# A linear-attention and gated-MLP kernel on one core: decays scanned over whole units, 48-column loads, another layout of x, other fillers on TensorE, and a re-planned order

## The chip, the cores and the metric

The kernel runs on one core of a Trainium2 chip. The metric is the device time of one execution in microseconds; the shown runs of the kernel before took 529.38, 530.78 and 531.95 us, median 530.78.

## The reference

Four batches of eight heads run a recurrence over 768 tokens; its output, laid out as 3072 tokens of 384 features, goes through two matrix products with a piecewise quadratic gate between them.

```python
for t in range(S):
    y[:, :, t] = einsum('bhd,bhde->bhe', rt, state + (u * kt) x vt)
    state = wt[:, :, :, None] * state + kt x vt
x = y.transpose(0, 2, 1, 3).reshape(3072, 384)
h = x @ w_in                                    # 384 -> 2048
g = where(h >= 1, h, where(h <= -1, 0, (h + 1) ** 2 / 4))
out = g @ w_out                                 # 2048 -> 384
```

## The kernel before

**Units.** The tokens are cut into 12 units of 256 (`UT`), three to a batch; a unit is four chunks of 64 (`C`). Two units make a block of 512 tokens, and the products run block by block.

**Attention of a unit** (`attention`). The decays w of a unit come in two halves q (pairs of heads, 128 partitions). For each half VectorE scans w to running products p (L405), takes the reciprocal of the last (L399), scans backwards to y (L400), and multiplies k by y (L428) and r by p (L478). Each chunk of 64 has its own start of the scan. TensorE then multiplies 64x64 tiles: `among` (L448) gives r times k within a chunk, in the first four units a second time with u times k (L416 on GpSimd, `with_u`); `ktrans` (L487) transposes k; `umat` (L509) makes k times v per chunk. VectorE picks masked parts of the `among` products (L454, `picked`), and builds the states at the chunk borders from `umat`: per chunk an add (L527) and a multiply by the chunk's total decay (L528), `chain`. At the end `cross` and `along` (both L550) add up state times r and picked scores times v into two banks of PSUM. ScalarE and VectorE evacuate these into `x` as a high part and a rest (L606, L604), and six small transfers fill in the rows of the last head (L649). Unit 0 has a path of its own (`ALONE`): matmuls L625 and L616 take the place of the transfers and of VectorE's rest.

**Weights.** Each of 16 slices f of the two weight matrices is loaded as 64-bit numbers (768 KB) and decoded: ScalarE (L329, L326, L322), GpSimd (L330, `rr`), VectorE (L332 `fl`, then L335 `wt`, the low part). The tile `rr` exists once, so GpSimd's L330 for one slice waits until VectorE's L332 for the slice before has read it.

**Products.** For every block and slice, nine matmuls of 512 columns make h (L896, `product_in`), five operations on ScalarE and VectorE gate it (L712, L713, L714 `g`, L716 `gh`, L717 `gl`), and nine more add into the output banks (L916, `product_out`, whose last three wait for `gl`). Some steps of the first two blocks run in two halves of 256 columns, so that they can start when only one unit of the block is there: 112 steps in all.

**The order.** Nothing is issued as it is written: every operation is recorded in a `Plan` with an engine, a cost in us, the tiles it touches and a due time. The planner plays a list schedule with these costs and emits all engines' instructions in the order found; each engine then works strictly in that order. Due times come from constants: `LEADS` by unit, `DECODE` for the weights, `STEP`, `FIRST` and `PACED` for the products. `kept_warm` puts matmuls on zeros (L304) into TensorE's queue where the planner sees a gap longer than `IDLE`; `warm` (L298) is eight of these at the start.

Of the kernel before, what the change touches and what calls it, by code (L numbers as in the profile page):

```python
# [26 lines left out]
SEG = 2 * NC * (C + 1)  # L27
# [22 lines left out]
class Plan:  # L50
# [7 lines left out]
    HOP = 0.15  # L58
# [4 lines left out]
    def add(self, engine, cost, emit, due, reads=(), writes=(), port=False, size=0, fresh=True):  # L63
# [37 lines left out]
    def kept_warm(self, order, engine, banks, fill):  # L101
# [4 lines left out]
        for n in order:  # L106
            op = ops[n]
            if op["e"] == engine:
# [8 lines left out]
                free = begin[n] + op["cost"]  # L117
# [3 lines left out]
    def order(self):  # L121
# [24 lines left out]
        while any(open_.values()):  # L146
# [66 lines left out]
STEP, FIRST, PACED = 4.9, 24.0, 4.6  # L213
# [3 lines left out]
def attention_moe(tc, a):  # L217
# [63 lines left out]
    for t, v, name in ((zero, 0.0, "zero"), (seeds, 0.0, "seeds"), (minus_one, -1.0, "minus_one")):  # L281
        op("POOL", 0.5, SOON, (), [name], lambda t=t, v=v: G.memset(t, v))
# [17 lines left out]
    op("PE", 2.0, SOON, ["zero"], [("b", 6)], warm)  # L300
# [8 lines left out]
    def weight(f, when):  # L309
# [20 lines left out]
        op("POOL", 2.0, due, [("raw", f)], ["rr_high"], lambda: G.tensor_scalar(  # L330
# [6 lines left out]
        plan.group(first, when, DECODE)  # L337
# [12 lines left out]
    def attention(u, when):  # L350
# [45 lines left out]
        def scan(q, back):  # L396
            w = wq[slot[q]]
            if back:
                V.reciprocal(seeds[:, :, C], pv[:, q, :, C])  # L399
# [3 lines left out]
            else:  # L403
                V.memset(seeds[:, :, C], 0.0)
# [15 lines left out]
        for q in (1, 0):  # L420
            s = slot[q]
            if early:
                op("POOL", 1.6, due, [("k", s), "cst"], [("ku", q), "nk"], lambda q=q: with_u(q))
            op("DVE", 1.3, due, [("w", s)], [("p", q), "seeds"], lambda q=q: scan(q, False), port=True)
            op("ACT", 0.2, due, [("p", q)], [("ptot", u, q)], lambda q=q: A.copy(
                ptot[:, 16 * u + 8 * q : 16 * u + 8 * q + 8], pv[:, q, :, C]))
            op("DVE", 1.45, due, [("w", s), ("p", q)], ["y", "seeds"], lambda q=q: scan(q, True), port=True)
            op("DVE", 0.69, due, ["y"], [("k", s)], lambda q=q: V.tensor_tensor(  # L428
                out=parts(q, 1), in0=parts(q, 1), in1=y_.rearrange("p (n c) -> p n c", c=C + 1)[:, :, 1:], op=ALU.mult), port=True)
# [47 lines left out]
        for q in (1, 0):  # L477
            op("DVE", 0.69, due, [("p", q)], [("r", slot[q])], lambda q=q: V.tensor_tensor(  # L478
                out=parts(q, 0), in0=parts(q, 0), in1=pv[:, q, :, 0:C], op=ALU.mult), port=True)
# [505 lines left out]
```

## Time and profile before

| | before |
|---|---|
| median of the runs shown | 530.78 us |
| span of the profiled execution | 526.9 us |
| median less this span | 3.9 us |
| TensorE matmuls, busy | 503.0 us, 95% of the span |
| VectorE, busy | 340.4 us, 65% |
| ScalarE, busy | 294.4 us, 56% |
| GpSimd, busy | 108.8 us, 21% |
| transfers, moved | 54.22 MB, mean 103 GB/s |

The profile is of one execution. PE is TensorE's matmuls, PEld its weight loads, DVE VectorE, ACT ScalarE, POOL GpSimd, SP SyncE, which issues the transfers. L numbers are lines of the kernel. A group's row has busy time and mean duration of one, then the idle time of the engine just before these instructions and who ended it. An fp32 matmul of the attention appears as two records, the products' matmuls as one. Matmuls overlap, so a mean duration is longer than the distance from one to the next; the chain of waits shows that distance.

### The profile page before, as it was taken

The page shows a single profiled execution, that of the slowest core. Times are in us where ns is not written, and L with a number is a line of the kernel's source. Part 1 is how long each engine was busy: PE and PEld are TensorE (multiplying, and loading weights), DVE is VectorE, ACT ScalarE, POOL GpSimd, SP SyncE. Part 2 cuts the span into 40 slices and gives each one's busy share as a digit, 9 for nine tenths or more (in the row PEclk, how much of TensorE's full clock was granted, in tenths as well). Part 3 has the DMA queues.
Part 4 walks back from the last instruction along what each step waited for, and adds up shares of the span by engine and source line. Part 5 has one row for each costly group of instructions (what it writes and reads, how often), then busy time and mean ns, then how long its engine had stood idle before and what let it go on. Part 6 is the DMA issues. An engine that isn't in the chain of part 4 may idle for free.

```text
span 526.9 us, 12832 instructions
## 1 busy us (share of the span) xinstructions
PE 503.0 (95%) x5438; PEld 412.2 (78%) x5438; DVE 340.4 (65%) x592; ACT 294.4 (56%) x596; POOL 108.8 (21%) x76
## 2 busy tenths in 40 slices
PE   7778899999999999999999999999999999999993
PEld 5557787788999988887877778887787777788882
DVE  5989799999897868324398869445833545333331
ACT  1387698878786556433464736443744444444441
POOL 6496865740203021000111011101000100000000
PEclk9899999999999999999999999999999999999997
DMA  8865472344835171100234404103200100100001
GB/s 321 344 240 179 152 318 81 122 148 145 271 104 181 44 237 48 61 0 3 82 125 140 151 20 151 56 2 109 78 0 2 41 17 12 66 0 1 0 0 67
DMA packets 21921, 54.22 MB, mean 103 GB/s; under 512 B 3104, under 2 KB 8672, under 8 KB 21856
## 3 DMA queue, kind: packets, MB, share of 16 engines
q1 hardware_dynamic: 21568, 52.93, 29.2%
q8 instruction: 44, 0.72, 0.5%
q10 hardware_dynamic: 288, 0.39, 0.2%
q14 instruction: 21, 0.17, 0.1%
HBM read 46.43 MB, written 4.72 MB: 97 GB/s over the span
## 4 chain that ended last, share of the span: by engine, by line
PE 77%; POOL 6%; DVE 5%; issue 4%; DMA 3%; ACT 1%; SPq 1%; ACTq 0%; DVEq 0%; POOLq 0%
PE h L896 35%; PE acc L916 33%; POOL rr L330 4%; PE bank L550 3%; POOL nk L416 3%; PE bank L509 2%; PE bank L448 2%; PE bank L487 1%; DMA rk<-in_rk 1%; DVE fl L332 1%; SPq L649 1%; DMA cst<-in_consts 1%; DVE y L400 1%; DVE p L405 1%; DVE gl L717 1%
## 5 line engine op out<-in xcount | busy, mean ns | idle before, releaser
L896 PE MATMUL h<-x,wt 128*128 128x512 f32 (+1 forms) x1008 | 223.7, 367 | 2.4 <-DVE wt L335 1.5
L896 PEld LDWEIGHTS h<-x,wt 128*128 128x128 f32 x1008 | 169.6, 188 | 36.2 <-DVE wt L335 2.2
L916 PE MATMUL acc<-gh,wt 128*128 128x512 f32 (+1 forms) x672 | 156.4, 368 | 0.0
L714 DVE SCALAR_TENSOR_TENSOR g<-g,h 128x512 f32<-128x512 f32 (+1 forms) x112 | 67.9, 606 | 99.8 <-ACT g L713 97.5
L916 PEld LDWEIGHTS acc<-gh,wt 128*128 128x128 f32 x672 | 114.0, 188 | 22.1 <-issue 0.5
L712 ACT ACTIVATE g<-h 128x512 f32<-128x512 f32 (+1 forms) x112 | 60.0, 536 | 116.6 <-PE h L896 113.4
L717 DVE TENSOR_TENSOR gl<-g,gh 128x512 fp32r<-128x512 f32 (+1 forms) x112 | 71.5, 640 | 35.6 <-ACT gh L716 35.6
L916 PE MATMUL acc<-gl,wt 128*128 128x512 f32 (+1 forms) x336 | 86.1, 364 | 1.1 <-DVE gl L717 1.1
L716 ACT CAST gh<-g 128x512 fp32r<-128x512 f32 (+1 forms) x112 | 62.2, 556 | 44.4 <-DVE g L714 42.1
L916 PEld LDWEIGHTS acc<-gl,wt 128*128 128x128 f32 x336 | 58.7, 188 | 12.5 <-DVE gl L717 1.5
L713 ACT ACTIVATE g<-g 128x512 f32<-128x512 f32 (+1 forms) x112 | 63.9, 571 | 3.2
L474 POOL TENSOR_TENSOR r<-cst,d 128x512 f32<-128x512 f32 x16 | 16.8, 1070 | 227.5 <-PE bank L550 207.9
L330 POOL TENSOR_SCALAR rr<-wraw 128x768 uint16<-128x768 f32 x16 | 51.6, 3227 | 28.4 <-DVE fl L332 25.1
L405 DVE TENSOR_TENSOR_SCAN p<-wq,seeds 128x520 f32<-128x520 f32 x24 | 30.8, 1283 | 3.1 <-DMA wq<-in_w 2.3
L400 DVE TENSOR_TENSOR_SCAN y<-wq,seeds 128x520 f32<-128x520 f32 x24 | 30.4, 1266 | 0.8
L466 POOL TENSOR_TENSOR nk<-nk 128x768 f32<-128x768 f32 x8 | 15.3, 1914 | 52.5 <-DMA nk<-in_nk 52.5
L416 POOL TENSOR_SCALAR nk<-rk,cst 128x256 f32<-128x256 f32 x16 | 22.5, 1417 | 3.4 <-DMA cst<-in_consts 2.6
L428 DVE TENSOR_TENSOR rk<-rk,y 128x512 f32<-128x512 f32 x24 | 17.9, 745 | 3.6 <-POOL nk L416 2.3
L329 ACT ACTIVATE rr<-wraw 128x768 uint16<-128x768 uint32 x16 | 17.4, 1085 | 1.1 <-DMA wraw<-in_wbits 1.1
L550 PEld LDWEIGHTS bank<-rk,st 64*64 64x64 f32 x656 | 12.3, 134 | 6.9 <-issue 3.7
L454 DVE COPY_PREDICATED r<-below,bank 128x512 f32<-128x512 int32 x22 | 15.1, 727 | 4.0 <-PE bank L448 4.0
L478 DVE TENSOR_TENSOR rk<-rk,p 128x512 f32<-128x512 f32 x24 | 17.4, 736 | 0.3 <-PE acc L448 0.3
(104 smaller groups left out, 398.7 us busy)
## 6 DMA issues: line engine op xcount, KB each, us to landing
rk<-in_rk SPq DMA_DIRECT2D x24, 512.0 KB, 4.6
wraw<-in_wbits SPq DMA_DIRECT2D x16, 768.0 KB, 7.1
wq<-in_w SPq DMA_DIRECT2D x24, 260.5 KB, 2.8
nk<-in_nk SPq DMA_DIRECT2D x8, 768.0 KB, 4.6
vn<-in_v SPq DMA_DIRECT2D x11, 384.0 KB, 6.7
fl<-in_w SPq DMA_DIRECT2D x12, 260.0 KB, 3.1
out_y<-g SPq DMA_DIRECT2D x10, 256.0 KB, 2.5
x<-last SPq DMA_DIRECT2D x66, 32.0 KB, 2.9
```

The lines of the kernel that those rows point to most:

```text
L330: op("POOL", 2.0, due, [("raw", f)], ["rr_high"], lambda: G.tensor_scalar(out=r16[:, :, 1], in0=wraw[f][:, :, 1].bitcast(F32), scalar1=0.0 ...
L400: V.tensor_tensor_scan(out=y_[:, ::-1], data0=w[:, SEG:0:-1], data1=sv[:, ::-1], initial=0.0, op0=ALU.mult, op1=ALU.add)
L405: V.tensor_tensor_scan(out=pv[:, q].rearrange("p n c -> p (n c)"), data0=w[:, 0:SEG], data1=sv, initial=0.0, op0=ALU.mult, op1=ALU.add,)
L416: G.tensor_scalar(out=ku[:, q, cs], in0=rk[slot[q]][:, 1, cs], scalar1=u_col[:, 2 * q + pr : 2 * q + pr + 1], scalar2=None, op0=ALU.mult)
L550: PE.matmul(out=bank[by[g]][HP * half : HP * half + HP, lo : lo + C], start=first, stop=False, skip_group_check=True, **kw)
L712: op("ACT", c, due, [("b", 6 + hk)], [("g", gk)], lambda: nc.scalar.activation(gs, hs, AF.Relu, scale=0.5, bias=0.5))
L713: op("ACT", c, due, (), [("g", gk)], lambda: nc.scalar.activation(gs, gs, AF.Square))
L714: op("DVE", 0.13 + 0.53 * k, due, [("b", 6 + hk)], [("g", gk)], lambda: nc.vector.scalar_tensor_tensor(out=gs, in0=gs, scalar=1.0, in1=hs, ...
L716: op("ACT", c, due, [("g", gk)], [("gh", gk)], lambda: nc.scalar.copy(ghs, gs))
L717: op("DVE", 0.15 + 0.5 * k, due, [("g", gk), ("gh", gk)], [("gl", gk)], lambda: nc.vector.tensor_tensor(out=gls, in0=gs, in1=ghs.bitcast(F ...
L896: nc.tensor.matmul(hp, lhsT=wx[f][:, cs], rhs=xt[:, j, :], start=n == 0, stop=n == 8)
L916: nc.tensor.matmul(o[j], lhsT=wx[f][:, cs], rhs=gt, start=first and i == 0, stop=stop and i == 2, skip_group_check=True)
```

## The change

- **Decays.** The scans start once per unit and pair instead of once per chunk (`SEG` is 514 columns, not 520). The states then need no multiply per chunk: `chain` becomes one add (or one copy), and only the unit's last state is multiplied, by the unit's total (`carry`).
- **48 columns.** The left operands of `umat`, and of `cross` and `along` except in units 0 and 6, are 48 columns instead of 64.
- **x by chunk parity.** Each chunk's results go to a contiguous half of x; the output's tokens are put back in order on the host.
- **Unit 0's u times k** goes from GpSimd to ScalarE, in four instructions.
- **Fillers.** `zeros` and `warm` use an f32r tile `clear`, made by one copy on VectorE, in matmuls of 512 or 256 columns; `warm` is now 48 fp32 matmuls of 64x64 and one f32r matmul for each bank. `IDLE` falls from 1.0 to 0.5, and a gap is filled to 72%.
- **The planner** knows latencies, a price for changing between 64 and 128 row tiles, two rates of transfer; many costs are new, and all due times are.

```diff
-SEG = 2 * NC * (C + 1)
+SEG = 2 * (UT + 1)
-WARM = 8
-IDLE, ZEROS = 1.0, 1.2
+IDLE, FILLED, ZEROS = 0.5, 0.72, 0.235
+SMALL = 48
...
-    HOP = 0.15
+    HOP = 0.04
+    LATENCY = {"PE": 0.16, "DVE": 0.083, "ACT": 0.1}
+    LATE_64 = 0.31
+    TURN = {64: 0.22, 128: 0.09}
+    RATES, SETTLED = (315e3, 400e3), 8.5
...
-SLACK = 1.95
-LEADS = {0: 75.5, 1: 62.4, 2: 17.0, 3: 9.3, 4: 39.0, 5: 15.7, 6: 12.1, 7: 78.9, 8: 43.2, 9: -6.2, 10: 15.7, 11: -1.1}
-LEAD, DECODE = 15, 4.5
+SLACK = 0.501
+LEADS = {0: 89.12, 1: 29.14, 2: 50, 3: 29.29, 4: 70.5, 5: 42.42, 6: 96.05, 7: 79.29, 8: 141.79, 9: 131.35, 10: 73.56, 11: 100.77}
...
-STEP, FIRST, PACED = 4.9, 24.0, 4.6
+STEP, FIRST, PACED, AFTER = 17.0572, 293.658, 16.0129, 4.9
...
+    op("DVE", 0.2, SOON, ["zero"], ["clear"], lambda: V.tensor_copy(clear, zero))
     def warm():
-        for _ in range(WARM):
-            PE.matmul(hp[0][:, 0:128], lhsT=zero, rhs=zero, start=True, stop=True)
+        for n in range(SMALL):
+            g, h = n // 2 % 2, n % 2
+            PE.matmul(bank[h][HP * g : HP * g + C, 0:C], lhsT=zero[HP * h : HP * h + HP, 0:C], rhs=zero[HP * h : HP * h + HP, 0:C],
+                      start=True, stop=True)
+        for b in bank:
+            cleared(b, 4)
+    def cleared(out, n):
+        PE.matmul(out[:, 0 : 128 * n], lhsT=clear, rhs=clear.unsqueeze(1).broadcast_to([128, n, 128]), start=True, stop=True)
     def zeros(b, us):
-        for _ in range(int((us - 0.4) / ZEROS)):
-            PE.matmul(bank[b[1]], lhsT=zero, rhs=zero.unsqueeze(1).broadcast_to([128, 4, 128]), start=True, stop=True)
+        halves = int(FILLED * us / ZEROS * 2)
+        for i in range(0, halves, 2):
+            cleared(bank[b[1]], min(2, halves - i) * 2)
...
-                op("POOL", 1.6, due, [("k", s), "cst"], [("ku", q), "nk"], lambda q=q: with_u(q))
+                if alone:
+                    for pr in range(2):
+                        op("ACT", 0.42, due, [("k", s), "cst"], [("ku", q), "nk"], lambda q=q, pr=pr: A.activation(
+                            ku[:, q, pr * UT : pr * UT + UT], rk[slot[q]][:, 1, pr * UT : pr * UT + UT], AF.Copy,
+                            scale=u_col[:, 2 * q + pr : 2 * q + pr + 1]))
+                else:
+                    op("POOL", 2.85, due, [("k", s), "cst"], [("ku", q), "nk"], lambda q=q: with_u(q))
...
-                            i, o = slice(HP * g, HP * g + HP), slice(HP * h, HP * h + HP)
+                            i, o = slice(HP * g, HP * g + HP), slice(HP * h, HP * h + D)
...
-            V.tensor_tensor(out=sm, in0=up, in1=ss_(old), op=ALU.add)
-            V.tensor_tensor(out=out, in0=sm, in1=pt, op=ALU.mult)
+            if old is None:
+                V.tensor_copy(ss_(new), up(c))
+            else:
+                V.tensor_tensor(out=ss_(new), in0=up(c), in1=ss_(old), op=ALU.add)
+        def carry(new):
+            V.tensor_tensor(out=ss_(new), in0=sm, in1=ptot[:, 4 * u : 4 * u + 4].unsqueeze(2).broadcast_to([128, 4, D]), op=ALU.mult)
...
+        wide = HP if u in INPLACE else D
...
-                to = [x[:, n].rearrange("p a (c g t) -> p a c g t", c=2, g=2)[:, :, :, g, :] for n in range(2)]
+                to = [x[:, n, :, gs].rearrange("p a (c t) -> p a c t", c=2) for n in range(2)]
```

What stands in the queues is shown at three places. A row is line, operation, what is written from what is read, and the shape; the number behind a tile's name is its buffer, for `wraw` the slice f.

GpSimd's queue just behind the memsets of the start, before. `nk` from `rk` and `cst` is u times k of one half of a unit, `rr` from `wraw` is the step of decoding.

```order
L416 TENSOR_SCALAR nk0_84<-rk0_81,cst0_67 128x256 x2
L416 TENSOR_SCALAR nk0_84<-rk1_82,cst0_67 128x256 x2
L330 TENSOR_SCALAR rr0_115<-wraw0_170 128x768
L416 TENSOR_SCALAR nk0_84<-rk2_83,cst0_67 128x256 x2
L330 TENSOR_SCALAR rr0_115<-wraw1_181 128x768
L416 TENSOR_SCALAR nk0_84<-rk0_81,cst0_67 128x256 x2
L330 TENSOR_SCALAR rr0_115<-wraw2_192 128x768
L416 TENSOR_SCALAR nk0_84<-rk1_82,cst0_67 128x256 x2
L330 TENSOR_SCALAR rr0_115<-wraw3_313 128x768
```

The same place now:

```order
L358 TENSOR_SCALAR rr0_116<-wraw0_218 128x768
L358 TENSOR_SCALAR rr0_116<-wraw1_220 128x768
L444 TENSOR_SCALAR nk0_85<-rk2_84,cst0_67 128x256 x2
L358 TENSOR_SCALAR rr0_116<-wraw2_202 128x768
L444 TENSOR_SCALAR nk0_85<-rk0_82,cst0_67 128x256 x2
L358 TENSOR_SCALAR rr0_116<-wraw3_388 128x768
L444 TENSOR_SCALAR nk0_85<-rk1_83,cst0_67 128x256 x2
L358 TENSOR_SCALAR rr0_116<-wraw4_467 128x768
L358 TENSOR_SCALAR rr0_116<-wraw5_488 128x768
```

Unit 0's two rows are gone from the head of the queue, and slices 0 and 1 stand ahead of unit 1's rows.

VectorE's queue where unit 0's states are made, before; `ob`, `g` and `st` hold states, `bank` and `h` are PSUM.

```order
L525 TENSOR_TENSOR ob0_112<-h1_120,ptot0_76 128x4x48
L527 TENSOR_TENSOR sm0_99<-bank2_123,ob0_112 128x192
L528 TENSOR_TENSOR ob0_112<-sm0_99,ptot0_76 128x4x48
L527 TENSOR_TENSOR sm0_99<-h1_120,ob0_112 128x192
L528 TENSOR_TENSOR g2_105<-sm0_99,ptot0_76 128x4x48
L527 TENSOR_TENSOR sm0_99<-bank2_123,g2_105 128x192
L528 TENSOR_TENSOR st1_94<-sm0_99,ptot0_76 128x192
L454 COPY_PREDICATED r0_90<-below0_71,acc2_118 128x512
L454 COPY_PREDICATED r1_91<-below0_71,h0_119 128x512
```

And now:

```order
L488 COPY_PREDICATED r0_91<-below0_71,acc2_119 128x512
L488 COPY_PREDICATED r1_92<-below0_71,h0_120 128x512
L559 COPY ob0_113<-h1_121 128x4x48
L561 TENSOR_TENSOR ob0_113<-bank2_124,ob0_113 128x4x48
L561 TENSOR_TENSOR g2_106<-h1_121,ob0_113 128x4x48
L578 TENSOR_TENSOR sm0_100<-bank2_124,g2_106 128x192
L564 TENSOR_TENSOR st1_95<-sm0_100,ptot0_77 128x192
L360 SCALAR_TENSOR_TENSOR fl0_114<-fl0_114,rr0_116 128x768
```

Five instructions stand for seven, the picking moved ahead of them, and the decoding of slice 0 follows at once, ahead of unit 1's first scan.

TensorE's queue at the start, before:

```order
L298 MATMUL h0_119<-zero0_74 128x128 x8
L304 MATMUL bank0_121<-zero0_74 128x512 x4
L487 MATMUL bank0_121<-cst0_67,rk0_81 128x128 x4
L448 MATMUL acc0_116<-rk1_82,nk0_84 64x64
L448 MATMUL acc1_117<-rk1_82,nk0_84 64x64
```

And now, between the first fillers and the transposes of unit 0, with 46 more small matmuls and seven long ones where lines are left out:

```order
L325 MATMUL bank0_122<-clear0_75 128x512 x2
L319 MATMUL bank0_122<-zero0_74 64x64
L319 MATMUL bank1_123<-zero0_74 64x64
...
L325 MATMUL h1_121<-clear0_75 128x512
L325 MATMUL bank0_122<-clear0_75 128x512 x6
L521 MATMUL bank0_122<-cst0_67,rk0_82 128x128 x4
```

Ahead of the first real matmul stand 48 small and 16 long fillers instead of 8 and 4. In all there are 71 f32r fillers of 512 or 256 columns, 69 of them ahead of unit 2's first matmul; before there were 9 fp32 ones.

More of the change, by code (lines that the diff above doesn't have):

```diff
@@ L116, in kept_warm @@
                             break
-                free = begin[n] + op["cost"]
+                free = end[n] - self.late(op)
             out.append(op["emit"])
@@ L127, in order @@
                 users[m].append(n)
-        free, end, begin, lands = {}, {}, {}, []
+        free, end, begin, lands = {"SP": self.ISSUE}, {}, {}, []
         port = bus = 0.0
-        open_ = {}
+        mode = 128
+        ran = {}
+        open_ = {e: [] for e in ("PE", "SP", "ACT", "DVE", "POOL")}
         since = {}
@@ L135, in opened @@
             op = ops[n]
-            since[n] = max((end[m] + (0.0 if ops[m]["e"] == op["e"] and not ops[m]["size"] else self.HOP) for m in op["deps"]), default=0.0)
-            open_.setdefault(op["e"], []).append(n)
+            since[n] = max((ran[m] if ops[m]["e"] == op["e"] and not ops[m]["size"] else end[m] + self.HOP for m in op["deps"]), default=0.0)
+            open_[op["e"]].append(n)
         def ready(n):
@@ L524, in chain @@
             if old is None:
-                V.tensor_tensor(out=out, in0=up, in1=pt, op=ALU.mult)
-                return
-            V.tensor_tensor(out=sm, in0=up, in1=ss_(old), op=ALU.add)
-            V.tensor_tensor(out=out, in0=sm, in1=pt, op=ALU.mult)
-        for c in range(NC - (third == UB - 1)):
-            old, new = before[-1], (state["st"] + 1) % STATES
-            if alone and c < NC - 1:
+                V.tensor_copy(ss_(new), up(c))
+            else:
+                V.tensor_tensor(out=ss_(new), in0=up(c), in1=ss_(old), op=ALU.add)
@@ L533, in attention @@
+        def carry(new):
+            V.tensor_tensor(out=ss_(new), in0=sm, in1=ptot[:, 4 * u : 4 * u + 4].unsqueeze(2).broadcast_to([128, 4, D]), op=ALU.mult)
+        for c in range(NC - 1):
+            old = before[-1]
+            if alone:
                 new = list(wide_st)[c]
             else:
-                state["st"] = new
-            op("DVE", 0.35 if old is None else 0.71, due, [("b", bu[c % 2]), ("ptot", u, 0), ("ptot", u, 1)] + ([("s", old)] if old is not None else []),
-               [("s", new), "sm"], lambda c=c, old=old, new=new: chain(c, old, new), port=True)
+                new = state["st"] = (state["st"] + 1) % STATES
+            op("DVE", 0.36, due, [("b", bu[c % 2])] + ([("s", old)] if old is not None else []), [("s", new)],
+               lambda c=c, old=old, new=new: chain(c, old, new))
@@ L538, in attention @@
             before.append(new)
+        if third != UB - 1:
+            old = before[-1]
+            new = state["st"] = (state["st"] + 1) % STATES
+            op("DVE", 0.36, due, [("b", bu[1]), ("s", old)], ["sm"], lambda old=old: V.tensor_tensor(
+                out=sm, in0=up(NC - 1), in1=ss_(old), op=ALU.add))
+            op("DVE", 0.36, due, ["sm", ("ptot", u, 0), ("ptot", u, 1)], [("s", new)], lambda new=new: carry(new), port=True)
         by = [take(), take()]
         begun = set()
+        wide = HP if u in INPLACE else D
@@ L549, in put @@
             lo = ((pair // 2 * 2 + h) * 2 + c2) * C
-            PE.matmul(out=bank[by[g]][HP * half : HP * half + HP, lo : lo + C], start=first, stop=False, skip_group_check=True, **kw)
+            PE.matmul(out=bank[by[g]][HP * half : HP * half + wide, lo : lo + C], start=first, stop=False, skip_group_check=True, **kw)
         def inter(g, h, pair, c2):
```

128 lines of the change are left out of this document (70 added, 58 removed).

## The prediction

> **What bounds the kernel now.** I read the busy times by stretches first. The columns are the length, then the busy time of PE, PEld, DVE, ACT and POOL with their instructions, the granted clock, the share of the DMA engines and GB/s.
>
> ```profile
> 0.00:63.20 63.20, 49.15 (x882) 39.00 (x883) 50.29 (x86) 34.59 (x68) 45.20 (x42) 0.97 0.70 257
> 63.20:518.40 455.20, 453.80 (x4558) 373.20 (x4556) 289.65 (x506) 259.03 (x529) 63.64 (x35) 1.00 0.25 82
> 518.40:527.00 8.60, 0.00 (x0) 0.00 (x0) 0.42 (x1) 0.76 (x2) 0.00 (x0) 0.65 0.30 100
> ```
>
> From 63.2 us to 518.4 us TensorE stands for 1.4 us only; then 8.6 us go into the last output. So the end is set by two things: how much of TensorE's queue is done when the start lets go of it, and how long the queue itself is. The prices of its pieces stand in the chain of waits between 160 and 215 us (start, length, what):
>
> ```profile
> 166.01 1.05 PE acc L916 x9
> 167.07 1.09 PE bank L448 x64
> 168.16 1.27 PE acc L916 x9
> 169.43 0.44 PE bank L487 x4
> 173.46 1.08 PE bank L509 x64
> 180.02 0.63 PE bank L550 x32
> 182.96 1.56 PE bank L550 x96
> 191.04 4.21 PE h L896 x18
> ```
>
> A product of nine matmuls costs 1.05 us in half width and 2.1 us in full; the first one behind attention 1.27 us, so a change from 64-row to 128-row tiles costs 0.2 us. A unit's attention is 1.09 (`among`), two times 0.44 (`ktrans`), 1.08 (`umat`), 0.63 (`cross`) and 1.56 us (`along`).
>
> Now the start. The same view by line, up to 63.2 us, gives what TensorE had done; the rows are L896, L916, L448, L487, L509 and L550 in this order (first number: busy PE, in brackets the records). Two rows of the groups by line, for unit 0 alone, follow.
>
> ```profile
> 0.00:63.20 63.20, 10.97 (x72) 9.38 (x73) 0.97 0.70 257
> 0.00:63.20 63.20, 8.44 (x54) 6.98 (x54) 0.97 0.70 257
> 0.00:63.20 63.20, 6.77 (x320) 5.58 (x320) 0.97 0.70 257
> 0.00:63.20 63.20, 2.62 (x16) 1.68 (x16) 0.97 0.70 257
> 0.00:63.20 63.20, 2.30 (x128) 2.05 (x128) 0.97 0.70 257
> 0.00:63.20 63.20, 5.70 (x240) 5.10 (x240) 0.97 0.70 257
> ```
>
> ```profile
> L625 PE MATMUL acc<-g,nk 128*128 128x128 f32 x12 | 1.6, 284 | 0.4 <-ACT g L630 0.4
> L616 PE MATMUL acc<-x,minus 128*128 128x128 f32 x6 | 1.1, 292 | 0.1
> ```
>
> That is 8 products into h and 6 out of it, the sixth of which waits in its middle for `gl`: 13 x 1.06 = 13.8 us; 5 `among` 5.4; 4 `ktrans` 1.8; 2 `umat` 2.2; the `cross` and `along` of units 0 and 1 (240 of 256 records) 4.1; and 2.7 for unit 0's own matmuls. Together 30.0 us of work by 62.7 us: 32.7 us are lost, to fillers, waits and latency. What is lost here is never made up, because TensorE is full from then on.
>
> VectorE sets this loss. The sixth `gl` ends at 62.7 us, and it stands in the queue behind the decoding of a slice that came late from GpSimd:
>
> ```profile
> 61.41 0.96 DVE L332 SCALAR_TENSOR_TENSOR fl<-fl,rr 128x768 int32<-128x768 int32 x1 [2.10 <-POOL rr L330]
> 62.28 0.42 DVE L717 TENSOR_TENSOR gl<-g,gh 128x256 fp32r<-128x256 f32 x1
> 0.00:62.70 62.70, 48.71 (x879) 38.56 (x879) 49.82 (x84) 34.09 (x67) 44.70 (x42) 0.97 0.70 259
> 0.00:69.83 69.83, 55.78 (x927) 45.08 (x928) 56.92 (x98) 41.12 (x81) 50.14 (x43) 0.98 0.69 255
> ```
>
> Up to there VectorE worked 49.8 us and stood 12.9; up to 69.83 us, where the tenth `gl` ends, it worked 56.9 and stood no more. So the loss is VectorE's work ahead of a `gl`, less TensorE's work ahead of the same product, plus VectorE's idle time: 49.8 - 30.0 + 12.9 = 32.7. Where it stood tell the groups of its instructions up to 70 us (the last column is the idle time before them):
>
> ```profile
> L400 DVE TENSOR_TENSOR_SCAN y<-wq,seeds 128x520 f32<-128x520 f32 x6 | 8.0, 1338 | 0.2
> L405 DVE TENSOR_TENSOR_SCAN p<-wq,seeds 128x520 f32<-128x520 f32 x6 | 7.7, 1285 | 2.4 <-DMA wq<-in_w 2.3
> L332 DVE SCALAR_TENSOR_TENSOR fl<-fl,rr 128x768 int32<-128x768 int32 x8 | 7.7, 963 | 2.4 <-POOL rr L330 2.4
> L335 DVE TENSOR_TENSOR wt<-fl,wt 128x768 fp32r<-128x768 f32 x8 | 7.6, 955 | 1.0 <-ACT wt L322 1.0
> L428 DVE TENSOR_TENSOR rk<-rk,y 128x512 f32<-128x512 f32 x6 | 5.0, 838 | 2.3 <-POOL nk L416 2.3
> L714 DVE SCALAR_TENSOR_TENSOR g<-g,h 128x256 f32<-128x256 f32 x10 | 4.1, 411 | 1.4 <-ACT g L713 1.4
> L478 DVE TENSOR_TENSOR rk<-rk,p 128x512 f32<-128x512 f32 x4 | 2.6, 684 | 0.3 <-PE acc L448 0.3
> L454 DVE COPY_PREDICATED r<-cst,bank 128x512 f32<-128x512 int32 x3 | 2.2, 736 | 0.0
> L528 DVE TENSOR_TENSOR st<-sm,ptot 128x192 f32<-128x192 f32 x5 | 1.8, 358 | 0.2
> L454 DVE COPY_PREDICATED r<-below,h 128x512 f32<-128x512 int32 x1 | 0.7, 729 | 0.4 <-PE h L448 0.4
> L404 DVE MEMSET seeds<- 128x8 f32 x6 | 0.4, 65 | 1.6 <-POOL minus_one L282 1.5
> ```
>
> **The change, part by part.** The sum is made against the profiled span of 526.9 us; the median of the runs is 3.9 us above it, and I carry that over.
>
> *The start.* Counted along the new order up to the tenth `gl`, VectorE has these more than before: one scan each way (1.3 + 1.3), three pickings (2.2), two products of r (1.4), one low part of a slice (1.0), a reciprocal and the copy for `clear` (0.4 together, from like rows); and five state operations fewer (1.8). That is 5.8 us more, 62.7. TensorE has ahead of that product 10 half products in and one whole (12.7), 9 half products out (9.5), 6 `among` (6.5), 6 `ktrans` (2.6), 2 `umat` (2.0), 4.1 and 2.7 as before: 40.1 us. The loss is then 62.7 - 40.1 = 22.6 us plus the idle time. At the sixth `gl` before it was 19.8 plus 12.9. So the new order leans more on VectorE, by 2.8 us, and gains only by what VectorE waits less; it breaks even at 10.1 us of idle time.
>
> Of the idle time, 4.0 us (first memset, first load) stay. The 2.3 us behind `nk` come in part from unit 0, whose u times k moves to ScalarE. On GpSimd these four instructions held the queue for 5.4 us; an activation of the same shape takes 0.42 us on ScalarE, where little else runs then:
>
> ```profile
> 6.14 5.41 POOL L416 TENSOR_SCALAR nk<-rk,cst 128x256 f32<-128x256 f32 x4 [2.56 <-DMA cst<-in_consts]
> 32.35 0.42 ACT L713 ACTIVATE g<-g 128x256 f32<-128x256 f32 x1
> ```
>
> GpSimd is then free for the slices two rows earlier, and most of the 2.4 us behind `rr` should go; but its next u times k rows now stand behind two slices. The 1.4 us behind `g` follow from TensorE's waiting and shrink with it; the stop of 0.4 us behind L448 may return. I take 7.5 us, nearer to the 4.0 that stay than to the 12.9 of now; the ends are 4.9 and 12.9. The loss becomes 30.1 us (27.5 to 35.5): a gain of 2.6 us, between 5.2 gained and 2.8 lost.
>
> *`umat` in 48 columns.* `among` moves 64 columns and `umat` 48, both load 64, and both cost the same (1.09 and 1.08), so the load sets the price. Between `cross` and `along` 64 more records cost 0.93 us, so 0.93 of the 1.08 us scales. How a load scales shows in the weight loads:
>
> ```profile
> L896 PEld LDWEIGHTS h<-x,wt 128*128 128x128 f32 x1008 | 169.6, 188 | 36.2 <-DVE wt L335 2.2 <-DMA x<-last 1.3 <-issue 0.5
> L509 PEld LDWEIGHTS bank<-vn,kt 64*64 64x64 f32 x704 | 11.3, 134 | 4.1 <-issue 1.8 <-ACT kt L494 0.9 <-ACT gh L716 0.4
> ```
>
> Between 128 and 64 columns lie 54 ns, 0.84 ns a column; 16 columns less would take 134 ns to 120, a tenth: 0.09 us a unit, 1.1 us over 12. The other end is in proportion, a quarter: 0.23 us a unit, 2.8 us. I take 2.0, as spacing rather than latency is at stake. The Trainium skill, page "TensorE: Matmul & The Clock Gate", section on LDWEIGHTS, puts a load at its columns divided by 1.2 in ns, which is the quarter: by it this term is 2.8 us. Its slope (0.83 ns) agrees with the trace, its 107 ns for 128 columns do not.
>
> *`cross` and `along`.* Here the moving side stays at 64. If the load alone sets the price, 0.09 to 0.47 us a unit go (1.86 us scale), for ten units up to 4.7 us; if 64 moving columns bind next, nothing. No row separates them; I take 0.5.
>
> *Changes of tile size.* The new order goes into 64-row tiles 52 times, the old one 49 times: 3 x 0.2 = 0.6 us lost.
>
> *At nothing:* the contiguous x (same shapes, same engines), the check's fewer columns, the fillers and SyncE's order. The fillers cost up to 0.23 us each (a ninth of 2.1 us); they stand in gaps that VectorE's lag covers, and 29 of them come behind the first product: 6.8 us if that cover were gone. On SyncE slice 2 now goes ahead of unit 0's v, which is read by `umat`; if v came late it would count as idle time of VectorE, which the range holds. In 19.2 to 22.7 us the clock was halved:
>
> ```profile
> 19.20:22.70 3.50, 3.44 (x58) 2.07 (x60) 3.28 (x7) 1.21 (x4) 0.58 (x1) 0.51 0.92 356
> ```
>
> That is 1.7 us of TensorE, under VectorE's lag (3.28 of 3.50 us busy); that fillers may avoid it is put at nothing.
>
> The sum: 2.6 + 2.0 + 0.5 - 0.6 = 4.5 us; the span 522.4 us, the median 526.3 us. Later stops (1.4 us after 63.2) I leave as they are.
>
> **The rivals.** *Loads carry more.* `cross` and `along` are bound by loads too: 4.7 instead of 0.5, and `umat` 2.8: median 521.3 us; with the best start 518.7. For it speaks that `among` and `umat` cost the same; against it, that nothing shows a moving side of 64 to be free.
>
> *The start gives nothing.* VectorE idles about 10 us again, at other places: 2.0 + 0.5 - 0.6 remain, 528.9 us; and if shorter loads don't shorten the spacing, the change does there what it says and buys nothing: 530.9. For it speaks that `fl`, `wt` and `rk` each had their wait, and a strict queue finds new ones.
>
> *VectorE waits for slices, and it is slower.* Eight `fl` stand in its queue ahead of the tenth `gl`, with scans, pickings and gates behind each. Should six of them wait 2.1 us, as the one at 61.41 did, idle is 4.0 + 12.6 = 16.6 us, the loss 39.2, and the median 530.8 + 6.5 - 1.9 = 535.4 us. It is slower by over 0.5% (2.65 us, about what a measurement here can tell from no change) from 14.7 us of idle time. Against it speaks that GpSimd has two rows less ahead of slice 0.
>
> **How the numbers follow.** My forecast gets 0.54, more from loads 0.10, nothing from the start 0.24, slower 0.12. The first two are faster by over 0.5% (under 528.1), the third within it. The range runs from 519.5, near the best loads and start together, to 533, where the start loses its 2.8 us and `umat` gains 1.1.
>
> **What would show it.** By the windows of the changed kernel: VectorE's idle time up to its tenth `gl` (7.5 us; 10 or more proves the second rival, 15 the third), that `gl` at about 70 us, TensorE full from there on; `umat` at 0.9 us and `along` at 1.5 in the chain of waits; `nk` no longer a releaser in the first 12 us. If TensorE stands after 70 us for more than 3 us in all, the forecast is wrong at the point where I called the queue full.

## The result, and the profile after

| | before | after |
|---|---|---|
| median of five runs each, us | 529.38 (528.83 to 531.95) | 525.99 (525.05 to 526.38) |
| ratio after to before | | 0.992, 95% interval 0.990 to 0.995 |
| span of the profiled execution, us | 526.9 | 523.0 |
| TensorE's last matmul ends, us | 518.4 | 515.6 |
| tenth `gl` ends, us | 69.83 | 69.22 |
| VectorE's idle time up to there, us | 12.9 | 5.9 |

The change gains 0.8%, 3.4 us by the medians. The median is 0.3 us from the forecast of 526.3 us, but that forecast took 4.5 us off a median of 530.78, and the kernel before measured 529.38 here. So the closeness is in part luck, and the terms of the sum did not all come out either. The first view is again the busy time by stretches (length, then PE, PEld, DVE, ACT, POOL, the granted clock, DMA share, GB/s).

```profile
63.20:515.60 452.40, 447.77 (x4474) 366.28 (x4472) 275.69 (x467) 254.09 (x519) 65.04 (x34) 1.00 0.24 78
515.60:523.00 7.40, 0.00 (x0) 0.00 (x0) 0.42 (x1) 0.73 (x2) 0.00 (x0) 0.67 0.34 115
0.00:69.22 69.22, 63.52 (x1142) 54.12 (x1143) 63.34 (x104) 44.57 (x89) 46.35 (x39) 1.00 0.71 261
19.20:22.70 3.50, 3.50 (x90) 3.30 (x82) 3.46 (x4) 2.62 (x7) 3.50 (x1) 1.00 1.06 405
```

Behind 63.2 us TensorE now stands for 4.6 us (452.40 less 447.77), where it stood for 1.4. The halved clock at 19.2 to 22.7 us is gone. VectorE worked 63.3 us up to the tenth `gl` and stood 5.9. The groups of its instructions up to 70 us say where (last column); `nk` is no releaser any more, and `rr` holds `fl` for 1.0 us, not 2.4:

```profile
L433 DVE TENSOR_TENSOR_SCAN p<-wq,seeds 128x514 f32<-128x514 f32 x7 | 9.3, 1327 | 2.4 <-POOL st L312 2.1
L360 DVE SCALAR_TENSOR_TENSOR fl<-fl,rr 128x768 int32<-128x768 int32 x9 | 8.9, 986 | 1.0 <-POOL rr L358 1.0
L512 DVE TENSOR_TENSOR rk<-rk,p 128x512 f32<-128x512 f32 x6 | 4.0, 713 | 0.4 <-PE acc L482 0.4
L314 DVE CAST clear<-zero 128x128 fp32r<-128x128 f32 x1 | 0.5, 546 | 1.0 <-POOL zero L300 1.0
```

But no product waited for the tenth `gl`. TensorE's last stop ahead of 70 us is at 54.90 us, for unit 1's transfers into `x`; its last filler there begins at 51.17, and from 54.90 to 69.22 us it is busy for 14.29 of 14.32 us. In the kernel before a `gl` did hold it: of the 1.1 us in the second row, which is a group of the kernel before up to 63.2 us, 0.86 stand in front of the sixth, at 62.76.

```profile
54.90 2.37 PE L939 MATMUL h<-x,wt 128*128 128x256 f32 x18 [0.48 <-DMA x<-last]
```

```profile
L916 PE MATMUL acc<-gl,wt 128*128 128x256 f32 x18 | 3.3, 292 | 1.1 <-DVE gl L717 1.1
```

The chain of waits has the new prices of `umat` and `along`:

```profile
201.08 0.86 PE bank L543 x64
251.88 1.49 PE bank L592 x96
```

And TensorE's waits from 70 us on (in all, times, longest):

```profile
PE h L939 <- DVE g L756: 1.4, 4, 0.7
PE bank L521 <- DVE last L647: 1.3, 1, 1.3
PE bank L482 <- DVE rk L512: 0.9, 1, 0.9
PE bank L543 <- ACT gh L758: 0.3, 1, 0.3
PE bank L592 <- DVE st L561: 0.2, 1, 0.2
```

Besides, two fillers at 376.8 us take 0.9 us of TensorE. These stops are what the forecast did not have; three views say where they come from. At 130 us ScalarE waits 2.5 us in front of a gate (L754) for a transfer out that still reads `g`. What stands behind it is late by that, the evacuation into `last` too, and TensorE waits 1.3 us for it at 136 us:

```profile
125.19 0.60 ACT L776 COPY g<-acc 128x512 f32<-128x512 f32 x1
132.49 0.38 ACT L754 ACTIVATE g<-h 128x256 f32<-128x256 f32 x1 [2.53 <-DMA out_y<-g]
135.91 0.44 ACT L649 CAST last<-bank 128x128 fp32r<-128x128 f32 x2
```

This block's transfers out took up to 6.2 us to land, beside loads for the kernel's test of the decays' range (L710 and L711 on ScalarE, two activations for each of twelve loads, at 107 to 148 us). TensorE's 0.9 us in front of L482, at 119 us, lie beside these tests too. At 166 us a scan on VectorE takes 2.73 us instead of 1.23; beside it GpSimd runs its product of r and k:

```profile
165.66 2.73 DVE L428 TENSOR_TENSOR_SCAN y<-wq,seeds 128x514 f32<-128x514 f32 x1
```

```profile
165.47 1.83 POOL L500 TENSOR_TENSOR nk<-nk 128x768 f32<-128x768 f32 x1 [0.82 <-DMA nk<-in_nk]
```

GpSimd ends at 167.30, and the scan 1.09 us behind that, nearly the 1.23 us that it takes alone: it ran almost wholly once GpSimd was done. The same stands at 186 us (2.57 for 1.23) and 243 us (2.28 for 0.68), and TensorE stood for 0.27, 0.28 and 0.69 us right behind these three. The Trainium skill, page "SBUF — State Buffer", section "SBUF: two separate sides", says that the port pair shared by VectorE and GpSimd is locked for a whole instruction; the trace agrees.

### The profile page after: what moved, and what is told of

It reads as the page before. It is cut to its first block, busy times and chain, and to the rows that moved or that the text cites. A ratio compares the mean times of both kernels' runs of the same rounds, so it can differ in the third digit from the quotient of the medians.

```text
span 523.0 us, 13092 instructions
## 1 busy us (share of the span) xinstructions
PE 505.3 (97%) x5571; PEld 414.8 (79%) x5571; DVE 333.5 (64%) x561; ACT 294.0 (56%) x600; POOL 108.2 (21%) x72
## 4 chain that ended last, share of the span: by engine, by line
PE 62%; DVE 14%; ACT 8%; DMA 7%; issue 4%; POOL 3%; SPq 2%; ACTq 0%; DVEq 0%; POOLq 0%
PE acc L959 28%; PE h L939 28%; PE bank L592 3%; POOL rr L358 3%; DMA rk<-in_rk 2%; DVE fl L360 2%; DMA wraw<-in_wbits 2%; DVE r L488 2%; DVE p L433 2%; DVE rk L512 1%; DMA x<-last 1%; DVE y L428 1%; PE bank L482 1%; DVE g L756 1%; DMA out_y<-g 1%
## 5 line engine op out<-in xcount | busy, mean ns | idle before, releaser
L754 ACT ACTIVATE g<-h 128x512 f32<-128x512 f32 (+1 forms) x112 | 59.7, 533 | 93.2 <-PE h L939 85.9
L759 DVE TENSOR_TENSOR gl<-g,gh 128x512 fp32r<-128x512 f32 (+1 forms) x112 | 73.1, 655 | 36.6 <-ACT gh L758 35.8
L959 PEld LDWEIGHTS acc<-gl,wt 128*128 128x128 f32 x336 | 58.5, 188 | 11.6 <-DVE gl L759 0.8
L358 POOL TENSOR_SCALAR rr<-wraw 128x768 uint16<-128x768 f32 x16 | 55.1, 3441 | 31.7 <-DVE fl L360 17.2
L508 POOL TENSOR_TENSOR r<-cst,d 128x512 f32<-128x512 f32 x16 | 18.9, 1202 | 174.9 <-PE bank L592 134.5
L433 DVE TENSOR_TENSOR_SCAN p<-wq,seeds 128x514 f32<-128x514 f32 x24 | 31.5, 1313 | 3.1 <-POOL st L312 2.1
L428 DVE TENSOR_TENSOR_SCAN y<-wq,seeds 128x514 f32<-128x514 f32 x24 | 31.5, 1312 | 0.8
L500 POOL TENSOR_TENSOR nk<-nk 128x768 f32<-128x768 f32 x8 | 16.8, 2101 | 64.9 <-DMA nk<-in_nk 57.7
L528 ACT COPY kt<-bank 128x512 f32<-128x512 f32 x24 | 13.8, 583 | 17.8 <-PE bank L521 17.8
L325 PE MATMUL bank<-clear 128*128 128x512 f32 (+1 forms) x60 | 17.6, 411 | 1.6 <-DVE seeds L432 1.6
L592 PEld LDWEIGHTS bank<-rk,st 48*48 48x48 f32 (+1 forms) x656 | 11.5, 121 | 7.8 <-issue 2.2
```

The costliest lines, as they stand in the source:

```text
L358: op("POOL", 3.2, due, [("raw", f)], ["rr_high"], lambda: G.tensor_scalar(out=r16[:, :, 1], in0=wraw[f][:, :, 1].bitcast(F32), scalar1=0.0 ...
L428: V.tensor_tensor_scan(out=y_[:, ::-1], data0=w[:, SEG:0:-1], data1=sv[:, ::-1], initial=0.0, op0=ALU.mult, op1=ALU.add)
L433: V.tensor_tensor_scan(out=pv[:, q].rearrange("p n c -> p (n c)"), data0=w[:, 0:SEG], data1=sv, initial=0.0, op0=ALU.mult, op1=ALU.add,)
L592: PE.matmul(out=bank[by[g]][HP * half : HP * half + wide, lo : lo + C], start=first, stop=False, skip_group_check=True, **kw)
L754: op("ACT", c, due, [("b", 6 + hk)], [("g", gk)], lambda: nc.scalar.activation(gs, hs, AF.Relu, scale=0.5, bias=0.5))
L759: op("DVE", 0.15 + 0.54 * k, due, [("g", gk), ("gh", gk)], [("gl", gk)], lambda: nc.vector.tensor_tensor(out=gls, in0=gs, in1=ghs.bitcast( ...
```

## The experiments

Each kernel was timed in five rounds (two, named below, in three). The kernel before had medians of 529.4 to 530.6 us in the five sessions, so kernels of different sessions compare to about 1 us; what is finer is read from the traces.

**The loads.** Three kernels take them apart: the 48 columns alone in the old order (`b_48`), and 64 columns again in the new order in `umat` or in `cross` and `along`.

```diff
 b_48 (kernel before)
-  i, o = slice(HP * g, HP * g + HP), slice(HP * h, HP * h + HP)
+  i, o = slice(HP * g, HP * g + HP), slice(HP * h, HP * h + (HP if u in ALONE else D))
...
+  wide = HP if u in INPLACE else D
...
+  put(g, pair, h, c2, lhsT=vs(i, c2, 2 * pair + h, wide), rhs=r_[h][i, pair, c2, :])
 a_umat64 (kernel after)
-  i, o = slice(HP * g, HP * g + HP), slice(HP * h, HP * h + D)
+  i, o = slice(HP * g, HP * g + HP), slice(HP * h, HP * h + HP)
 a_y64 (kernel after)
-  wide = HP if u in INPLACE else D
+  wide = HP
```

> The kernel before, in its own order, with the 48-column left operands alone: umat in all units but unit 0, cross and along in all but units 0 and 6. Theory (the loads carry their part wherever they stand): in the two traces umat costs 1.08 us before and 0.87 after, cross and along together 2.19 and 2.11. So 10 units of umat behind the start give 2.05 us, 9 or 10 of cross and along 0.8 us: the median falls by 2.8 us. Rival 1 (the slope of the load durations alone, 0.84 ns a column): 1.1 us. Rival 2 (prices fell because the new order groups the work otherwise): no change. Rival 3 (in the old order the time that comes free turns into waits for VectorE behind 140 us): under 1 us, with new stops of TensorE of about 2 us.

> The changed kernel with 64-column left operands in umat again, same order. Theory: umat goes from 0.87 back to 1.08 us, 2.05 us for the ten units behind the start, and some of it is absorbed by TensorE's stops after 70 us (4.5 us in all): the median rises by 1.5 to 2.0 us. Rival (prices follow the order): no change.

> The changed kernel with 64-column left operands in cross and along again, same order. Theory: 0.08 us a unit, 0.5 to 0.8 us slower. Rival 1 (the moving side of 64 columns binds, and the 0.08 us have another cause): no change. Rival 2 (loads set all of it, a quarter of 1.86 us a unit): 4 us slower.

Measured: `b_48` 527.08 us against 530.52 (ratio 0.994, 0.992 to 0.996); `a_umat64` 527.63 (0.995, 0.993 to 0.997); `a_y64` 526.33 (0.993, 0.991 to 0.996). The windows of one line alone give the price: TensorE's busy time in `umat` and in `cross` with `along` for the nine units behind 120 us. Kernel before, lines L509 and L550:

```profile
120.00:522.00 402.00, 10.33 (x576) 9.22 (x576) 1.00 0.22 72
120.00:522.00 402.00, 20.89 (x1104) 18.43 (x1104) 1.00 0.22 72
```

Kernel after, L543 and L592:

```profile
120.00:522.00 402.00, 8.41 (x576) 7.33 (x576) 1.00 0.22 71
120.00:522.00 402.00, 20.15 (x1104) 17.50 (x1104) 1.00 0.22 71
```

`b_48`, L509 and L552:

```profile
120.00:522.00 402.00, 8.41 (x576) 7.30 (x576) 1.00 0.22 72
120.00:522.00 402.00, 20.10 (x1104) 17.45 (x1104) 1.00 0.22 72
```

`a_umat64`, L543, and `a_y64`, L592:

```profile
120.00:522.00 402.00, 10.33 (x576) 9.25 (x576) 1.00 0.22 71
```

```profile
120.00:522.00 402.00, 20.94 (x1104) 18.47 (x1104) 1.00 0.22 71
```

The price goes with the columns, in the old order and in the new: 1.92 us over nine units, 0.21 a unit, in `umat`; 0.74 to 0.79, 0.08 a unit, in the other two. Against the 525.99 us of the kernel after, `a_umat64` is 1.6 us up, as expected; the 0.3 us of `a_y64` can't be told from nothing by the medians. In the old order the 48 columns alone bring 3.4 us of median, as much as the whole change: by the sum at the end, what the new order gains at the start it loses again behind it.

**The fillers.** One kernel leaves the new fillers out of the new order (those of the first 9 us stay), one puts them into the old order.

```diff
 a_nofill (kernel after)
-  halves = int(FILLED * us / ZEROS * 2)
+  halves = 0
 b_fill (kernel before)
-IDLE, ZEROS = 1.0, 1.2
+IDLE, FILLED, ZEROS = 0.5, 0.72, 0.235
...
+  PE.matmul(bank[b[1]][:, 0 : 128 * n], lhsT=clear, rhs=clear.unsqueeze(1).broadcast_to([128, n, 128]), start=True, stop=True)
```

> The changed kernel without the zero matmuls in gaps (those of the first 9 us stay), same order of everything else. Theory (as forecast: fillers stand in gaps that VectorE's lag covers): the tenth gl ends where it did, 69.2 us, and nothing is lost; the two fillers at 376.8 us (0.87 us) go, 0 to 0.9 us faster. Rival (fillers hold the clock): the granted clock falls to half for 3 us or more after each pause of TensorE in the first 55 us, TensorE loses 1.7 us or more there where it is waited for, and the tenth gl ends 1 to 3 us later; 1 to 3 us slower.

> The kernel before, in its own order, with the changed kernel's fillers alone: f32r zeros of 512 or 256 columns in every gap of the plan over 0.5 us, filled to 72%. Theory (without fillers the changed kernel lost 3.8 us and its clock was halved in four stretches; so fillers carry much of the start): the halved clock at 19.2 to 22.7 us goes, the tenth gl ends 1.5 to 3 us before 69.8 us, the median falls by 1.5 to 3 us. Rival 1 (my forecast: fillers stand under VectorE's lag and are worth nothing): no change, tenth gl at 69.8 us. Rival 2 (fillers ahead of products that are waited for cost more than they give): tenth gl later, median up by 1 to 2 us.

Measured: `a_nofill` 529.76 us, spread from 525.82 to 533.17 (0.999, 0.997 to 1.001); `b_fill` 529.55 (0.999, 0.998 to 1.000). Windows of `a_nofill`, the first up to its tenth `gl`:

```profile
0.00:76.63 76.63, 55.33 (x1077) 49.14 (x1078) 62.89 (x104) 44.40 (x89) 46.08 (x39) 0.89 0.65 236
10.00:14.00 4.00, 3.73 (x72) 2.93 (x72) 3.19 (x6) 1.28 (x3) 0.00 (x0) 0.58 1.05 421
20.00:28.00 8.00, 6.67 (x85) 6.14 (x85) 7.11 (x8) 4.72 (x10) 8.00 (x4) 0.57 0.95 340
57.00:66.70 9.70, 5.78 (x86) 5.52 (x87) 5.08 (x10) 3.24 (x7) 3.87 (x4) 0.65 0.73 268
```

The rival holds: the clock is halved in three stretches (from 10.7, 20.9 and 58.5 us), VectorE stands 13.7 us (76.63 less 62.89) instead of 5.9, and the tenth `gl` is 7.4 us late in this execution, which is one of the longer ones. Of these, 2.6 us are there when unit 1 is evacuated (its first L647 starts at 50.22 us, not 47.66), behind two of the three stretches. The rest comes at 57 us, where TensorE stands 4.0 us for unit 1's transfers into x and then works at half clock:

```profile
PE h L939 <- DMA x<-last: 4.0, 1, 4.0
```

Why these transfers landed late here is open; stops of this kind may be what spreads the runs over 7 us. By the medians the fillers are worth 3.8 us. Without them the new order is slower than `b_48`, which has the same loads in the old order (but for unit 0's `umat`). Windows of `b_fill`:

```profile
0.00:69.90 69.90, 63.47 (x979) 55.39 (x980) 57.41 (x99) 41.00 (x81) 49.42 (x43) 0.95 0.69 256
17.00:20.60 3.60, 2.82 (x23) 2.32 (x24) 2.90 (x6) 0.00 (x0) 2.08 (x3) 0.57 1.04 394
55.00:58.30 3.30, 3.30 (x50) 3.14 (x43) 2.42 (x4) 0.95 (x1) 2.70 (x3) 0.51 0.95 340
```

In the old order the same fillers do nothing: VectorE stands 12.5 us, as before, and the tenth `gl` ends at 69.90. The clock still halves twice there: the fillers stand in the gaps of the plan, and TensorE stood elsewhere too (1.36 and 1.02 us, at 51.8 and 53.6 us, ahead of the second fall). So the fillers pay in the new order, and the new order needs them. That they act through the clock alone is not shown.

**The two edits that spare VectorE** (three rounds each): unit 0's u times k back on GpSimd, and an extra instruction per state in the place of the multiply that whole-unit decays save.

```diff
 a_gps (kernel after)
-  ku[:, q, pr * UT : pr * UT + UT], rk[slot[q]][:, 1, pr * UT : pr * UT + UT], AF.Copy,
-  scale=u_col[:, 2 * q + pr : 2 * q + pr + 1]))
+  out=ku[:, q, pr * UT : pr * UT + UT], in0=rk[slot[q]][:, 1, pr * UT : pr * UT + UT],
+  scalar1=u_col[:, 2 * q + pr : 2 * q + pr + 1], scalar2=None, op0=ALU.mult))
 a_mult (kernel after)
   V.tensor_tensor(out=ss_(new), in0=up(c), in1=ss_(old), op=ALU.add)
+  V.tensor_tensor(out=ss_(new), in0=ss_(new), in1=ss_(new), op=ALU.max)
```

> The changed kernel with unit 0's u times k on GpSimd again, at the same place of the order. Theory: k times y writes over the k that u times k reads, so VectorE waits for it as it did before (2.3 us behind nk): the idle time up to the tenth gl rises from 5.9 to about 8 us, the tenth gl ends 1.5 to 2.3 us later, the median rises by 1.5 to 2.3 us. Rival (GpSimd stands idle from 10 to 14 us in the changed kernel, so the four instructions find room there, and unit 0 has slack elsewhere): no change.

> The changed kernel with one more VectorE instruction behind every state that is added up (the state with itself, maximum, which changes no value; 0.36 us each, 32 in all, five of them ahead of the tenth gl), in the place of the multiply that whole-unit decays save. Theory (each us of VectorE's work ahead of the tenth gl is one us of the end): tenth gl 1.8 us later, median up by 1.8 us, and up to 1 us more from stops behind 70 us. Rival (VectorE's idle time of 5.9 us takes it up): tenth gl where it was, no change.

Measured: `a_gps` 526.49 us (0.993, 0.990 to 0.995), `a_mult` 535.60 (1.009, 1.007 to 1.012). VectorE's waits in `a_gps` up to 71 us have the old releaser back:

```profile
DVE rk L462 <- POOL nk L453: 1.8, 1, 1.8
```

In its profiled execution the tenth `gl` ends 1.8 us late, at 71.05; the median, 0.5 us up, does not tell the two cases apart. In `a_mult` it ends at 70.97 us, 1.75 late where 1.8 was expected. VectorE's work up to there grew by 2.6 us (the added instructions and 0.8 us of longer ones), and its idle time took up 0.9 (70.97 less 65.96 is 5.0):

```profile
0.00:70.97 70.97, 62.71 (x1138) 53.55 (x1139) 65.96 (x110) 44.26 (x89) 46.91 (x39) 1.00 0.70 255
```

But the median is up by far more than either case gave. TensorE's waits from 70 us on, in `a_mult`:

```profile
PE bank L593 <- DVE st L562: 6.7, 9, 1.8
PE h L940 <- DVE g L757: 3.2, 4, 1.2
```

With smaller ones they are 12.3 us in all, against 4.1 in the kernel after. In nine places `cross` waits for a state. The states of a unit hang on each other, between `umat` and `cross`, and the new order has put only as many products between the two as the short chain needs. In this order the shorter chain is worth more than VectorE's time in it.

**The late stops.** First the twelve loads and tests are moved behind 205 us, every other engine's order kept:

```diff
 a_late (kernel after)
+  order = [n for n in plan.best(step_ops, dues) if not any(n in h for h in held)]
+  for i, h in enumerate(held):
+      at = order.index(step_ops[48 + 2 * i])
+      order[at + 1 : at + 1] = list(h)
```

> The changed kernel with the twelve loads and checks of the first six units' decays (24 activations on ScalarE, 3 MB of transfers) moved from 107 to 148 us to 205 to 325 us; every other engine's order is kept. Theory (ScalarE's queue between 107 and 137 us makes TensorE's stops there: 0.94 us at 119 us behind a gh that stands behind checks, 1.7 us at 129 to 137 us behind a transfer out that shares the wires with these loads): the first goes, the second shrinks below 1 us; median down by 1.5 to 2.5 us. Rival (VectorE's own work sets these stops): they stay, no change.

Measured: 534.60 us (1.009, 1.007 to 1.012). Windows, and ScalarE at 215 us:

```profile
70.00:160.00 90.00, 89.90 (x1224) 77.17 (x1226) 76.00 (x136) 60.42 (x126) 33.98 (x14) 1.00 0.41 137
205.00:330.00 125.00, 115.86 (x1227) 91.67 (x1218) 77.31 (x134) 73.92 (x163) 14.71 (x11) 0.97 0.38 121
216.00:222.00 6.00, 4.65 (x73) 4.17 (x74) 3.56 (x6) 5.25 (x14) 0.94 (x1) 0.72 0.11 23
```

```profile
215.67 0.63 ACT L710 ACTIVATE fl<-fl 128x514 f32<-128x514 f32 x1 [4.69 <-DMA fl<-in_w]
```

Between 70 and 160 us TensorE stands 0.1 us; the kernel after stood 3.1 there (its row is below). So the cause was right, though how much of it is the loads and how much the tests is not told apart. But I had put each load directly ahead of its test: at 215 us ScalarE waits 4.7 us for the transfer, TensorE behind it 4.0, and the clock falls. From 205 to 330 us TensorE stands 9.1 us in all at a mean clock of 0.97: the edit, not the theory, cost the time. The next three put each load four product steps ahead of its test (and the first block's evacuations on ScalarE into free tiles), split GpSimd's product, and do both and leave out the two fillers at 376.8 us:

```diff
 a_late2 (kernel after)
+      at = order.index(step_ops[50 + 2 * i]) + 1
+      order[at:at] = h[1:]
+      at = order.index(held[i - 2][-1] if i > 1 else step_ops[46]) + 1
+      order.insert(at, h[0])
...
+  if j and b == 0:
+      o = fl[j - 1][:, 0:WIDE]
 a_split (kernel after)
+  out=nk[:, i // 2, 0, s], in0=nk[:, i // 2, 0, s], in1=nk[:, i // 2, 1, s], op=ALU.mult)
+  for i in range(4) for s in [slice(i % 2 * 192, i % 2 * 192 + 192)]], port=True)
 a_best (both, and no fillers behind 100 us)
-  if gap > IDLE:
+  if gap > IDLE and begin[n] < 100.0:
```

> As a_late, but each load now stands four product steps ahead of its check in the queues (in a_late it stood directly ahead, and ScalarE waited for it with products behind), and the first block's two evacuations on ScalarE go to free tiles of the decoding. Theory (the stops of 107 to 137 us come from these checks and loads, and what a_late lost it lost by ScalarE waiting for transfers): stops of TensorE behind 70 us fall from 4.6 to about 2 us, median down by 2 to 2.7 us against the changed kernel, 523.5 us. Rival (ScalarE has no room for the checks anywhere before 330 us): new stops of 2 us or more between 205 and 330 us, no gain.

> The changed kernel with GpSimd's product of r and k (128x768) in four pieces of 128x192. Theory (VectorE's instructions with two SBUF operands wait until GpSimd's running two-operand instruction ends: three of them took 1.5 to 1.6 us longer beside it at 166, 186 and 243 us, and TensorE stood 0.27, 0.28 and 0.69 us right behind): with pieces of 0.5 us the extra time falls under 0.6 us each, these three stops go, up to 1.2 us faster. Rival (GpSimd takes all its pieces before VectorE gets a turn): the three instructions are as long as before, no change.

> a_late2 and a_split together, and without the two fillers at 376.8 us. Theory (the three causes of late stops are independent): 2.0 to 2.7, 1.0 and 0 to 0.9 us: 521.5 to 523 us. Rival (the gains overlap, or the stop behind the last filler is there anyway): no more than 1 us better than the better of the two.

Measured: `a_late2` 523.93 us (0.989, 0.987 to 0.991), `a_split` 523.77 (0.989, 0.986 to 0.991), `a_best` 522.26 (0.986, 0.983 to 0.989). The kernel after, then `a_late2`, up to 160 us and from 285 to 330 us:

```profile
70.00:160.00 90.00, 86.90 (x1171) 73.50 (x1170) 72.61 (x130) 72.27 (x155) 33.47 (x13) 1.00 0.51 170
285.00:330.00 45.00, 45.00 (x419) 35.92 (x418) 26.80 (x46) 25.02 (x49) 2.53 (x2) 1.00 0.20 60
```

```profile
70.00:160.00 90.00, 89.89 (x1245) 77.17 (x1247) 75.94 (x137) 60.73 (x127) 34.85 (x15) 1.00 0.42 138
285.00:330.00 45.00, 43.10 (x408) 33.74 (x407) 25.96 (x45) 28.81 (x60) 2.08 (x2) 1.00 0.25 77
```

3.0 us are gained and 1.9 lost again at 285 to 330 us, where the tests now stand. In `a_split` VectorE's scan at 166 us takes 1.57 us beside GpSimd's pieces, not 2.73, and the second piece 1.52 us instead of 0.6:

```profile
166.54 1.57 DVE L428 TENSOR_TENSOR_SCAN y<-wq,seeds 128x514 f32<-128x514 f32 x1
```

The three stops behind such instructions are gone; the median moved by 2.2 us, which is more than they were (1.24), and the excess lies within what sessions differ by. `a_best` is better than the better of the two by 1.5 us, with the two fillers gone. Its stops left at 300 and 319 us led to the last kernel:

```diff
 a_best2 (as a_best)
-      at = order.index(step_ops[50 + 2 * i]) + 1
+      at = order.index(step_ops[68 + i]) + 1
...
-  if j and b == 0:
+  if j and b < 3:
```

> As a_best, but the twelve loads and checks stand one to a product step from about 315 us to 365 us, and the first three blocks' evacuations go to the free tiles. In a_best 1.46 us of TensorE's stops stood at 300 and 319 us: the first behind a transfer out that SyncE had issued late, the second behind checks on ScalarE. Theory (the checks only have to stand where ScalarE is free, and it is busiest before 330 us): both go, 1 to 1.5 us faster than a_best, 521 us. Rival (ScalarE is no freer at 315 to 365 us): new stops there, no gain.

Measured: 520.72 us (0.982, 0.979 to 0.985), faster than both kernels. Its waits of TensorE from 70 us on:

```profile
PE h L950 <- DVE g L757: 1.0, 1, 1.0
PE bank L593 <- ACT look L629: 0.8, 1, 0.8
PE bank L593 <- DVE st L562: 0.3, 1, 0.3
```

## Why the prediction held, and which of its steps did not

- **The start: 1 us short, and held elsewhere than I said.** By its own prices the loss at the tenth `gl` is 69.2 - 40.1 = 29.1 us against 32.7: a gain of 3.6, not 2.6. As I had built the sum, VectorE stood 5.9 us and not 7.5, and its work ahead (63.3) was counted well (62.7). But "VectorE sets this loss", through a `gl`, is true of the kernel before only. In the new one TensorE's last stop is at 54.90 us for unit 1's transfers into `x`, and as it loses nothing from there on, the sum gives the same at every later point. VectorE acts ahead of that: its evacuation of unit 1 (L647, 47.66 to 49.06 us) lets the transfers go. `a_mult` moves the tenth `gl` by 1.75 us for 1.8 us of added instructions, and the stop at 54.90 too, to 57.17; what VectorE's shorter waiting alone is worth in the end is not shown.
- **The fillers "at nothing": wrong.** I took their cover, VectorE's lag, from the old order. There it holds (`b_fill`). In the new order the clock halves at 10.7, 20.9 and 58.5 us without them, VectorE waits longer, and they are worth 3.8 us. Without them "the start gives nothing" would have come: 13.7 us of idle time in the profiled execution, over my 10.1 of break-even.
- **`umat`: right.** 0.21 us a unit, 2.6 over twelve, of which 2.1 behind the start; I took 2.0 between 1.1 and 2.8. A weight load of 48 columns takes 121 ns (134 with 64), as the slope said; yet the spacing fell by a fifth, near the quarter. So the distance from one load to the next scales with columns, though a load's duration has a constant part.
- **`cross` and `along`: right in kind.** 0.08 us a unit, 0.8 instead of 0.5. So the loads do not set most of this price; that the moving side of 64 columns does, as I had supposed, was not tried apart.
- **"TensorE full from there on": wrong**, by the mark I had set (3 us): it stands 4.6 us, and fillers take 0.9 more, against 1.4. The step that failed is "Later stops I leave as they are". The new order puts the decays' tests into ScalarE's fullest stretch, a transfer out beside their loads, and GpSimd's product beside VectorE's scans. `a_late` and `a_late2` show the first two together, the trace of `a_split` the third.
- **The end.** From TensorE's last matmul on it is 7.4 us, not 8.5 (7.1 to 7.4 in the other profiles of the new order, 8.1 and 8.4 in those of the old). I had not expected it, and its cause was not tried.
- **The sum.** Start 3.6, loads 2.1 and 0.8, the end 1.1, later stops and fillers -4.1: 3.5 of the 3.9 us by which the span fell; I had said 4.5. The rest holds the changes of tile size (-0.6 expected), which were not measured apart. The 3.9 us between span and median that I carried over compared two executions: run by run the kernel before lies 2.3 to 2.4 us above its span in the later sessions, and the five runs after 2.0 to 2.1. So errors met, and that the median came within 0.3 us is luck: the span came out 0.6 us above the forecast and the median execution another 0.9, and the carry was 1.9 us too high.

## What to carry to other kernels

A gain that is banked at the start reaches the end only if the engine that is full stays full: after a re-plan, read the stretches behind it for the engines that were not the bound, here ScalarE's queue and the port of VectorE and GpSimd. Side work with no due time belongs where its engine is free, its load well ahead, and never directly ahead of its use in a queue that others need. Whether fillers pay is asked of the new order, since the slack that covers a slow clock in the old one may be just what the new one takes away.

## What the runs showed of the hardware

- The granted clock halves behind pauses shorter than I had thought. In the kernel before it fell at 19.3 us, behind a single stop of 2.66 us at 15.9; in `b_fill` at 55.0 us, behind stops of 1.36 and 1.02 us at 51.8 and 53.6. Each fall lasts 3.3 us or more. The Trainium skill, page "TensorE: Matmul & The Clock Gate", Part 1, gives one idle window of about 3.4 us for it; here stretches of 3.4 us that were only partly idle were enough (0.8 us of work between 15.9 and 19.3 us). With the new fillers it never fell ahead of 70 us in any of the ten profiles of the new order.
- VectorE's scan waits for the whole GpSimd instruction, but gets a turn between two of them: 2.73 us beside one of 768 columns, 1.57 beside four of 192, of which the second took 1.52 us instead of 0.6.
